# A residual block on one core: constant products in TensorE's first gaps, later norm steps on GpSimd, both middle rows in one addition

## The chip, the core and the metric

The kernel runs on one core of one Trainium2 chip. The metric is the device time of one execution in microseconds (us). The engines are named as in the profile: PE (TensorE, matmuls; PEld are its weight loads), DVE (VectorE), ACT (ScalarE), POOL (GpSimd) and SP (SyncE, which here issues DMAs).

## What is computed

The reference is a residual block of a diffusion model, for two images of 512 channels and 64 x 64 points, in bf16:

```python
def gn(z, gamma, beta):                       # 4 groups of 128 channels
    zr = z.reshape(B, G, (C // G) * H * W)
    mu = zr.mean(-1).reshape(B, G, 1)
    var = ((zr - mu) ** 2).mean(-1).reshape(B, G, 1)
    zn = ((zr - mu) / jnp.sqrt(var + eps)).reshape(B, C, H, W)
    return zn * gamma.reshape(1, C, 1, 1) + beta.reshape(1, C, 1, 1)
...
h = conv3(_silu(gn(x, g1, be1)), w1)          # 3 x 3, 512 -> 512 channels, zero padding
emb = _silu(t_emb) @ w_emb
h = h + emb.reshape(B, C, 1, 1)
h = conv3(_silu(gn(h, g2, be2)), w2)
return x + h
```

## The kernel before

**Tiling.** Channels lie on the 128 partitions, so there are four channel tiles (ct for input, ot for output), and a norm's group is one such tile. Each image is cut into two chunks of 32 rows; with two images that makes four chunks per layer, handled in order. A chunk and an output tile make one set (`one_set`): 16 sets in each of two layers, the very last of which is written out apart (`final_set`).

**The convolution.** Rows are transformed in the manner of Winograd: four output rows come from six positions (`pos` 0 to 5). `v_block` makes the transformed input V of one channel tile: ACT's SiLU with the norm's scale `sc` and bias `nb` writes `a_tmp`, and DVE additions (with some ACT or DVE scalings) turn that into V. `u_blocks` transposes the weights on PE and makes the transformed weights U on DVE and ACT. PE then multiplies V by U in `row_pair` and `col_pair` (the matmuls of L645, 512 or 256 columns wide, into three PSUM accumulators `acc`). `one_set` puts the output rows together: ACT copies accumulators to `m1`, `w_` and `mb`, DVE forms sums and differences in `w_`, ACT scales two of them by 2 and by 4 into the halves of `m1`, and DVE adds these to `w_` and so writes the middle output rows 1 and 2 of every four (two additions of 512 elements), then rows 0 and 3.

**Norms.** Image 0's first norm (`first_stats`) gets its sums of squares from PE products of x with itself (L943), its means from ACT and DVE sums or from PE products with ones (L957). Image 1's (`second_stats`) comes from ACT and DVE sums over 4096 elements (L985). Layer 1's norms (`stats2`) come from sums that layer 0's steps leave behind. All end in `norm`: a product with `ones_neg` (L405) sums over partitions, DVE copies it (L409), and a row of steps on numbers of one column per group (tile `arena`) makes `sc` and `nb`; two of the kinds of step run on POOL, the addition of epsilon (L419) and the power of minus one half (L423), the others on DVE.

**Order.** No queue's order is written out by hand. Every step is added to `_Plan` with an engine, a modelled cost and latency, what it reads and writes, and for PE's matmuls a due time. `issue` schedules all engines by lists with random restarts and then emits each engine's instructions in the order found. An engine works its queue strictly in that order, so one changed step or cost can change the order of everything. In the profile, L320, L325, L333 and L350 are the helpers `tt`, `ts`, `stt` and `act`, which record most DVE and ACT steps; steps are told apart there by tiles.

Of the kernel before, what the change touches and what calls it, by code (L numbers as in the profile page):

```python
# [12 lines left out]
ALU = mybir.AluOpType  # L13
# [11 lines left out]
class _Plan:  # L25
# [33 lines left out]
    def region(self, a):  # L59
        if isinstance(a, str):  # L60
            return a, 1
        m = self.mask(a.offset, tuple((d[0], d[1]) for d in list(a.ap)[1:]))
        bank = self.banks.get(a.tensor.name)
        if bank:
            m = sum(1 << i for i in range(8) if (m >> (i * bank)) & ((1 << bank) - 1))
        return a.tensor.name, m
# [124 lines left out]
def kernel(  # L191
# [13 lines left out]
    nc = tc.nc  # L205
    P = nc.NUM_PARTITIONS
# [20 lines left out]
    SMALLS = 344  # L227
    PARAM_LAND = 5.5
    LATE = 4.0
    DVE_SUMS = (1,)  # L230
    COL0 = (1, 2, 3)
    POS_ORDER = (1, 3, 2, 4, 0, 5)
# [85 lines left out]
    def tt(out, in0, in1, op, **kw):  # L318
        plan.add("DVE", vcost("tt", (out, in0, in1)),
                 lambda: nc.vector.tensor_tensor(out=out, in0=in0, in1=in1, op=op), [in0, in1], [out], **kw)  # L320
# [73 lines left out]
    sc_all = {(l, b): small([CT], "sc") for l in range(2) for b in range(B)}  # L394
    nb_all = {(l, b): small([CT], "nb") for l in range(2) for b in range(B)}

    def norm(layer, b, c0, n, me, ps=None):
        bank = None
        if ps is None:
            bank = XBank("xb", [2 * n], F32)  # L400
        tok = ["xb"] if ps is None else []

        def mm():
            o = ps if ps is not None else bank.get()[:]
            nc.tensor.matmul(o, lhsT=ones_neg[:], rhs=me[:], start=True, stop=True)  # L405
        plan.add("PE", 0.15, mm, [me[:], ones_neg[:]], tok if ps is None else [ps], lat=0.2, lead=100.0,
                 wait=0.05 if ps is not None else LATE)
        tot = small([2 * n], "tot")
        plan.add("DVE", 0.1, lambda: nc.vector.tensor_copy(out=tot[:], in_=ps if ps is not None else bank.get()[:]),  # L409
                 tok if ps is None else [ps], [tot[:]])  # L410
        nvar, rstd = small([n], "nvar"), small([n], "rstd")
        mu, ex = tot[:, 0:n], tot[:, n:2 * n]
        if n == 1:
            stt(nvar[:], mu, mu, ex, ALU.mult, ALU.add)
        else:
            tt(nvar[:], mu, mu, ALU.mult)
            tt(nvar[:], nvar[:], ex, ALU.add)
        ts(nvar[:], nvar[:], 0.0, op=ALU.min)
        pool(lambda: nc.gpsimd.tensor_scalar(out=rstd[:], in0=nvar[:], scalar1=-1.0, scalar2=EPS,  # L419
                                             op0=ALU.mult, op1=ALU.add), [nvar[:]], [rstd[:]])  # L420
        for i in range(n):
            r = rstd[:, i:i + 1]
            pool(lambda r=r: nc.gpsimd.tensor_tensor(out=r, in0=r, in1=neg_half[:], op=ALU.pow), [r, neg_half[:]], [r])  # L423
        sc, nb = sc_all[layer, b][:, c0:c0 + n], nb_all[layer, b][:, c0:c0 + n]
        tt(sc, rstd[:], gam(layer)[:, c0:c0 + n], ALU.mult)
        if layer == 1:
            tt(mu, mu, emb_sb[:, b, c0:c0 + n], ALU.add)
        if n == 1:
            stt(nb, mu, sc, bet(layer)[:, c0:c0 + n], ALU.mult, ALU.add)
        else:  # L430
            tt(nb, mu, sc, ALU.mult)
            tt(nb, nb, bet(layer)[:, c0:c0 + n], ALU.add)

    Ut = [[[None] * CT for _ in range(CT)] for _ in range(2)]
    KP = NKX * P
# [338 lines left out]
    def one_set(layer, idx, ot, U, V):  # L774
        b, ch = chunks[idx]
        col = is_col(layer, b, ch)
        more = layer == 1 and idx >= len(chunks) - 2
        gid = (layer, idx, ot)
        rows = slice(ch * CR * W, (ch + 1) * CR * W)
        yst = next_y()  # L780
        y4 = yst[:].rearrange("p (t f w) -> p f t w", f=TH, w=W)
        base = sum(cols_of(b, c) for c in range(ch))
        acc_sum = lambda i: ssum[b][:, ot, base + i:base + i + 1]

        late = more and idx == len(chunks) - 1 and ot == 0

        def first_pair():
            if more:
                (more_cols(U, V, gid) if idx == len(chunks) - 2 else more_pair(U, gid))
            else:  # L790
                a = row_pair((1, 3), U, V, col, gid, 1)
                if layer == 0:
                    act(m1[:], a[:], func=ACT.Identity, scale=KAPPA, accum=acc_sum(0))
                else:
                    act(m1[:], a[:], scale=KAPPA)

        if not late:
            first_pair()
        if col:
            ab = col_pair((1, 2), U, V, gid)  # L800
            act(mb[:].rearrange("p k j n -> p j k n"), ab, scale=0.5)
        a = row_pair((2, 4), U, V, col, gid, 1)
        act(w_[:, 1], a[:], scale=KAPPA)
        if late:
            first_pair()
        if col:
            tt(sd[:, 0], mb[:, 0], mb[:, 1], ALU.add)
            tt(sd[:, 1], mb[:, 0], mb[:, 1], ALU.subtract)
        tt(w_[:, 0], m1[:], w_[:, 1], ALU.add)
        tt(w_[:, 1], m1[:], w_[:, 1], ALU.subtract)  # L810
        t1, s1, t2, s2 = w_[:, 0, 0], w_[:, 1, 0], w_[:, 0, 1], w_[:, 1, 1]
        if layer == 0:
            act(m1[:, 1], t2, func=ACT.Identity, scale=4.0, accum=acc_sum(1))
            act(m1[:, 0], s2, func=ACT.Identity, scale=2.0, accum=acc_sum(2))
        else:
            act(m1[:, 0], s2, scale=2.0)
            act(m1[:, 1], t2, scale=4.0)
        act(s2, s2, scale=8.0)
        z12 = t4(m1[:])
        tt(y4[:, 1], z12[:, 0], t4(w_[:, 1, 0:1])[:, 0], ALU.add)  # L820
        tt(y4[:, 2], z12[:, 1], t4(w_[:, 0, 0:1])[:, 0], ALU.add)
        tt(w_[:, :, 0], w_[:, :, 0], w_[:, :, 1], ALU.add)
        w03 = t4(w_[:, :, 0])
        if not col:
            a = row_pair((0, 5), U, V, col, gid, 1)
            m05 = view(sd, 0, [[NFREE, 2], [1, NFREE]])
            act(m05, a[:], func=ACT.Identity, accum=acc_sum(3))
            tt(y4[:, 0:TH:TH - 1], t4(m05), w03, ALU.add)
        else:
            aa = col_pair((0, 3), U, V, gid)  # L830
            if layer == 0:
                for j in range(2):
                    for k, op in ((0, 1.0), (1, -1.0)):
                        stt(view(yst, k + j * (TH - 1) * W, [[TH * W, TR], [2, W // 2]]),
                            aa[:, j, k].rearrange("p (t w) -> p t w", t=TR), op,
                            sd[:, k, j].rearrange("p (t w) -> p t w", t=TR), ALU.mult, ALU.add,
                            accum=acc_sum(3 + 2 * j + k), more=[aa])
            else:
                for k, op in ((0, ALU.add), (1, ALU.subtract)):
                    tt(view(yst, k, [[(TH - 1) * W, 2], [TH * W, TR], [2, W // 2]]),  # L840
                       sd[:, k].rearrange("p j (t w) -> p j t w", t=TR),
                       aa[:, :, k].rearrange("p j (t w) -> p j t w", t=TR), op)
        y03 = y4[:, 0:TH:TH - 1]
        if col:
            tt(y03, y03, w03, ALU.add)
        if layer == 0:
            dma(h_scr[b, ot][:, rows], yst[:], reads=[yst[:]], writes=[f"h{b}{ot}{ch}"])
            act(yst[:], yst[:], func=ACT.Square, scale=float(HW) ** -0.5, accum=ssq[b][:, ot, ch:ch + 1])
            return
        dma(yst[:], x_v[b, ot][:, rows], reads=[yst[:]], writes=[yst[:]], eng="POOL", accum=ALU.add)  # L850
        dma(out_v[b, ot][:, rows], yst[:], reads=[yst[:]], due=clock["t"] + 20)
# [67 lines left out]

    xt = [Vbuf[CT + ct][:, 0:HW] for ct in range(CT)]  # L920
    wload = [u_load(0, 0, ct, lead=900.0 - 200.0 * ct) for ct in range(2)]
    for ct in range(CT):
        n = 2 if ct in (0, CT - 1) else 1
        for k in range(n):
            o = xt[ct][:, k * HW // n:(k + 1) * HW // n]
            dma(o, x_v[0, ct][:, k * HW // n:(k + 1) * HW // n], writes=[o], lead=800.0 - 200.0 * ct)
# [6 lines left out]
    def first_stats(ct):  # L933
# [25 lines left out]
            plan.add("PE", 1.8, colsum, [xt[ct], ones_bf[:]], [cs], lat=0.2)  # L959
            act(cs, cs, func=ACT.Identity, scale=1.0 / (P * HW), accum=me[:, 0:1])  # L960
        stt(gr, gr, 1.0 / HW, ident[:], ALU.mult, ALU.mult, accum=me[:, 1:2])
        norm(0, 0, ct, 1, me, ps=st[:, 0, 0:2])

    for ct in range(CT):
        first_stats(ct)
# [11 lines left out]
    def second_stats(ct):  # L977
# [4 lines left out]
        for k in range(2):  # L982
# [4 lines left out]
            else:  # L987
                act(src[0][:, 0:HW // 2], xin, func=ACT.Identity, accum=part[:, k:k + 1])
            act(src[0][:, 0:HW // 2], xin, func=ACT.Square, scale=float(HW) ** -0.5, accum=part[:, 2 + k:3 + k])
        stt(me[:, 0:1], part[:, 0:1], 1.0, part[:, 1:2], ALU.mult, ALU.add)  # L990
        ts(me[:, 0:1], me[:, 0:1], 1.0 / HW)
        tt(me[:, 1:2], part[:, 2:3], part[:, 3:4], ALU.add)
        norm(0, 1, ct, 1, me)

    for layer in range(2):
# [74 lines left out]
```

## Time and profile before

| | |
|---|---|
| median of 3 runs | 503.36 us (503.23 to 503.74) |
| the profiled execution | 503.6 us, of which its span from first to last instruction 501.7 us |
| mean granted PE clock | 0.995 |
| busy: PE, DVE, ACT, POOL | 479.1, 468.2, 398.3, 38.4 us |
| first L645 matmul | at 21.4 us |
| HBM read, written | 38.22 MB, 16.78 MB |

Times within the profile are counted from the span's first instruction. A row of the timeline gives start, duration, engine, line, operation, the tile written and those read, and in brackets the idle time of the engine just before with what ended it. Instructions of one engine can overlap a little, so that from start to start is less than the mean duration.

### The profile page before, as it was taken

The page shows a single profiled execution, that of the slowest core. Times are in us where ns is not written, and L with a number is a line of the kernel's source. Part 1 is how long each engine was busy: PE and PEld are TensorE (multiplying, and loading weights), DVE is VectorE, ACT ScalarE, POOL GpSimd, SP SyncE. Part 2 cuts the span into 40 slices and gives each one's busy share as a digit, 9 for nine tenths or more (in the row PEclk, how much of TensorE's full clock was granted, in tenths as well). Part 3 has the DMA queues.
Part 4 walks back from the last instruction along what each step waited for, and adds up shares of the span by engine and source line. Part 5 has one row for each costly group of instructions (what it writes and reads, how often), then busy time and mean ns, then how long its engine had stood idle before and what let it go on. Part 6 is the DMA issues. An engine that isn't in the chain of part 4 may idle for free.

```text
span 501.7 us, 8355 instructions
## 1 busy us (share of the span) xinstructions
PE 479.1 (95%) x3081; PEld 285.8 (57%) x3082; DVE 468.2 (93%) x1054; ACT 398.3 (79%) x548; POOL 38.4 (8%) x97
## 2 busy tenths in 40 slices
PE   5888999999999999999999999999999999999994
PEld 4654554455554555555665655555555666768572
DVE  3988999999999999899999999999999999998576
ACT  4888999999985895999999999767667867526362
POOL 1120000000110002000000000040010000000000
PEclk9999999999999999999999999999999999999998
DMA  8433233641210333222643122453626642424354
GB/s 301 178 77 92 69 106 121 220 181 43 78 51 2 109 105 110 86 86 89 179 137 114 67 86 51 120 129 84 171 43 151 187 125 47 127 62 107 85 125 127
DMA packets 17315, 55.53 MB, mean 111 GB/s; under 512 B 1915, under 2 KB 3067, under 8 KB 16507
## 3 DMA queue, kind: packets, MB, share of 16 engines
q1 hardware_dynamic: 14912, 46.86, 27.5%
q0 software_dynamic: 2160, 7.87, 9.5%
q8 instruction: 24, 0.39, 0.4%
q10 hardware_dynamic: 203, 0.27, 0.1%
q14 instruction: 16, 0.13, 0.1%
HBM read 38.22 MB, written 16.78 MB: 110 GB/s over the span
## 4 chain that ended last, share of the span: by engine, by line
PE 51%; DVE 18%; ACT 5%; POOL 1%; issue 1%; DVEq 0%
PE acc L645 50%; DVE V L320 4%; DVE vt L320 4%; DVE w L320 2%; DVE y L320 2%; DVE y L333 2%; ACT U L495 1%; POOL arena L423 1%; DVE sd L320 1%; DVE arena L985 1%; ACT a_tmp L350 1%; DVE vt L325 1%; PE xa L389 1%; ACT m L350 1%; POOL arena L419 1%
## 5 line engine op out<-in xcount | busy, mean ns | idle before, releaser
L645 PE MATMUL acc<-V,U 128*128 128x512 bf16 (+1 forms) x2400 | 435.1, 338 | 7.0 <-DVE V L320 3.2
L645 PEld LDWEIGHTS <-U 128*128 128x128 bf16 x2592 | 250.2, 98 | 186.2 <-issue 9.5
L320 DVE TENSOR_TENSOR V<-vt 128x1056 bf16<-128x1056 bf16 (+2 forms) x132 | 90.3, 691 | 3.6 <-ACT vt L350 1.2
L350 ACT ACTIVATE m<-w 128x512 bf16<-128x512 bf16 x62 | 38.1, 636 | 14.7 <-DVE w L320 14.6
L350 ACT ACTIVATE w<-acc 128x1024 bf16<-128x1024 f32 (+1 forms) x32 | 32.5, 1016 | 19.2 <-PE acc L645 7.8
L320 DVE TENSOR_TENSOR w<-m,w 128x1024 bf16<-128x1024 bf16 (+1 forms) x63 | 42.7, 679 | 5.0 <-ACT w L350 4.6
L350 ACT ACTIVATE src<-vt 128x528 bf16<-128x528 bf16 x54 | 34.6, 650 | 15.5 <-DVE vt L320 15.3
L320 DVE TENSOR_TENSOR U<-U 128x768 bf16<-128x768 bf16 (+2 forms) x96 | 45.1, 483 | 0.7 <-ACT U L495 0.5
L350 ACT ACTIVATE a_tmp<-src,arena 128x2112 bf16<-128x2112 bf16 x20 | 43.0, 2152 | 2.7 <-DVE stage L320 2.7
L350 ACT ACTIVATE mb<-acc 128x1024 bf16<-128x1024 f32 x32 | 32.8, 1024 | 12.4 <-PE acc L645 8.1
L320 DVE TENSOR_TENSOR vt<-a_tmp 128x1056 bf16<-128x1056 bf16 x56 | 39.0, 700 | 0.7 <-ACT a_tmp L350 0.4
L389 PEld LDWEIGHTS <-stage 128*128 128x128 bf16 x288 | 26.5, 144 | 12.5 <-DMA stage<-in_w_dram 3.8
L350 ACT ACTIVATE y<-y 128x2048 bf16<-128x2048 bf16 x16 | 30.6, 1909 | 0.0
L495 ACT COPY U<-xa 128x768 bf16<-128x768 bf16 x31 | 25.6, 826 | 3.8 <-PE xa L389 3.7
L320 DVE TENSOR_TENSOR sd<-mb 128x512 bf16<-128x512 bf16 x64 | 25.8, 417 | 2.4 <-ACT mb L350 2.4
L350 ACT ACTIVATE m<-acc 128x1024 bf16<-128x1024 f32 x24 | 24.6, 1025 | 3.4 <-DVE y L320 3.3
L350 ACT ACTIVATE a_tmp<-V,arena 128x2112 bf16<-128x2112 bf16 x12 | 26.0, 2169 | 1.6 <-DVE arena L333 1.6
L320 DVE TENSOR_TENSOR y<-m,w 128x512 bf16<-128x512 bf16 x62 | 24.7, 416 | 1.1 <-ACT m L350 0.7
L368 POOL DMA_DIRECT2D y<-in_x_dram x15 | 13.2, 879 | 149.6 <-DVE y L320 128.6
L564 POOL MEMSET a_tmp<- 128x64 bf16 x32 | 5.2, 167 | 241.3 <-DVE vt L320 213.9
L320 DVE TENSOR_TENSOR vt<-vt,a_tmp 128x1056 bf16<-128x1056 bf16 x32 | 22.4, 701 | 0.9 <-ACT vt L350 0.9
L350 ACT ACTIVATE src<-V 128x2048 bf16<-128x2048 bf16 x12 | 22.9, 1906 | 0.0
(115 smaller groups left out, 504.6 us busy)
## 6 DMA issues: line engine op xcount, KB each, us to landing
stage<-in_w_dram SPq DMA_DIRECT2D x32, 288.0 KB, 2.8
src<-h_scr SPq DMA_DIRECT2D x16, 528.0 KB, 3.8
h_scr<-y SPq DMA_DIRECT2D x16, 512.0 KB, 3.0
y<-in_x_dram POOLq DMA_DIRECT2D x15, 512.0 KB, 5.6
out_dram<-y SPq DMA_DIRECT2D x15, 512.0 KB, 2.9
V<-in_x_dram SPq DMA_DIRECT2D x6, 1024.0 KB, 6.8
src<-in_x_dram SPq DMA_DIRECT2D x4, 528.0 KB
V<-in_x_dram SPq DMA_DIRECT2D x4, 512.0 KB, 6.9
```

The costliest lines, as they stand in the source:

```text
L320: lambda: nc.vector.tensor_tensor(out=out, in0=in0, in1=in1, op=op), [in0, in1], [out], **kw)
L325: nc.vector.tensor_scalar(out=out, in0=in_, scalar1=c, scalar2=None, op0=op)
L333: nc.vector.scalar_tensor_tensor(out=out, in0=in0, scalar=scalar, in1=in1, op0=op0, op1=op1, **extra)
L350: nc.scalar.activation(out=out, in_=in_, func=fn, scale=scale, **extra)
L368: q.dma_start(out=out, in_=in_, **extra)
L389: nc.tensor.transpose(sel(t), in_, ident[:in_.shape[0], :in_.shape[0]])
L419: pool(lambda: nc.gpsimd.tensor_scalar(out=rstd[:], in0=nvar[:], scalar1=-1.0, scalar2=EPS, op0=ALU.mult, op1=ALU.add), [nvar[:]], [rstd[:]])
L423: pool(lambda r=r: nc.gpsimd.tensor_tensor(out=r, in0=r, in1=neg_half[:], op=ALU.pow), [r, neg_half[:]], [r])
L495: lambda: nc.scalar.copy(out=out, in_=sel(bank.get())), [tok], [out])
L564: pool(lambda r=r: nc.gpsimd.memset(rows[:, r, 1:W + 1], 0.0), [], [rows[:, r, 1:W + 1]], cost=0.2)
L645: nc.tensor.matmul(ap, lhsT=l, rhs=r, start=k == 0, stop=k == total[key] - 1)
L985: plan.add("DVE", 2.18, lambda xin=xin, o=part[:, k:k + 1]: nc.vector.reduce_sum(out=o, in_=xin, axis=AX.X), [xin], [part[:, k:k + 1]])
```

## The change

It has four parts.

1. 23 groups of two 128 x 128 products of a tile of ones with itself are added for PE, into `acc[2]`, whose contents nothing reads; 11 of the groups depend on nothing else, 12 on the first weight block having landed.
2. The small steps of `norm` are written anew. The fused DVE steps (`stt`) become two plain ones each; the clamp takes the sign along, and the addition of epsilon is a POOL step of its own. With `quick=True` (image 0's first norms) the plain steps stay on DVE; otherwise they run on POOL. The planner's cost of a power step is 0.7 us instead of 0.45.
3. In `second_stats` three DVE steps become two POOL steps.
4. In `one_set` the two additions for output rows 1 and 2 become one of 1024 elements, which reads the two halves of `w_` with a negative step in its outermost dimension. `region`, with which the planner finds dependences, learns negative steps.

```diff
+        dims = [(d[0], d[1]) for d in list(a.ap)[1:]]
+        first = a.offset + sum(step * (n - 1) for step, n in dims if step < 0)
+        m = self.mask(first, tuple((abs(step), n) for step, n in dims))
...
+    WARM = (11, 12)
...
-        if n == 1:
-            stt(nvar[:], mu, mu, ex, ALU.mult, ALU.add)
-        else:
-            tt(nvar[:], mu, mu, ALU.mult)
-            tt(nvar[:], nvar[:], ex, ALU.add)
-        ts(nvar[:], nvar[:], 0.0, op=ALU.min)
-        pool(lambda: nc.gpsimd.tensor_scalar(out=rstd[:], in0=nvar[:], scalar1=-1.0, scalar2=EPS,
-                                             op0=ALU.mult, op1=ALU.add), [nvar[:]], [rstd[:]])
+        def two(out, in0, in1, op, fast=False):
+            if fast:
+                tt(out, in0, in1, op)
+            else:
+                pool(lambda: nc.gpsimd.tensor_tensor(out=out, in0=in0, in1=in1, op=op), [in0, in1], [out])
+
+        two(nvar[:], mu, mu, ALU.mult, quick)
+        two(nvar[:], nvar[:], ex, ALU.add, quick)
+        pool(lambda: nc.gpsimd.tensor_scalar(out=nvar[:], in0=nvar[:], scalar1=0.0, scalar2=-1.0,
+                                             op0=ALU.min, op1=ALU.mult), [nvar[:]], [nvar[:]])
+        pool(lambda: nc.gpsimd.tensor_scalar(out=rstd[:], in0=nvar[:], scalar1=EPS, scalar2=None, op0=ALU.add),
+             [nvar[:]], [rstd[:]])
...
-        tt(sc, rstd[:], gam(layer)[:, c0:c0 + n], ALU.mult)
+        two(sc, rstd[:], g_, ALU.mult, quick)
         if layer == 1:
-            tt(mu, mu, emb_sb[:, b, c0:c0 + n], ALU.add)
-        if n == 1:
-            stt(nb, mu, sc, bet(layer)[:, c0:c0 + n], ALU.mult, ALU.add)
-        else:
-            tt(nb, mu, sc, ALU.mult)
-            tt(nb, nb, bet(layer)[:, c0:c0 + n], ALU.add)
+            two(mu, mu, emb_sb[:, b, c0:c0 + n], ALU.add)
+        two(nb, mu, sc, ALU.mult, quick)
+        two(nb, nb, b_, ALU.add, quick)
...
-        tt(y4[:, 1], z12[:, 0], t4(w_[:, 1, 0:1])[:, 0], ALU.add)
-        tt(y4[:, 2], z12[:, 1], t4(w_[:, 0, 0:1])[:, 0], ALU.add)
+        tt(y4[:, 1:3], t4(m1[:]), view(w_, 2 * NFREE, [[-2 * NFREE, 2], [W, TR], [1, W]]), ALU.add)
...
+    for after in [()] * WARM[0] + [(wload[0][:, 0:1],)] * WARM[1]:
+        plan.add("PE", 0.2, lambda: [nc.tensor.matmul(acc[2][:, 1, 0:P], lhsT=ones_bf[:], rhs=ones_bf[:], start=True,
+                                                      stop=True) for _ in range(2)],
+                 [ones_bf[:]] + list(after), [acc[2][:]], group=("warm",), lat=0.1, due=4.0, lead=-100.0)
...
-        stt(me[:, 0:1], part[:, 0:1], 1.0, part[:, 1:2], ALU.mult, ALU.add)
-        ts(me[:, 0:1], me[:, 0:1], 1.0 / HW)
-        tt(me[:, 1:2], part[:, 2:3], part[:, 3:4], ALU.add)
+        pair = me[:, 0:2]
+        pool(lambda: nc.gpsimd.tensor_tensor(out=pair, in0=part[:, 0:4:2], in1=part[:, 1:4:2], op=ALU.add),
+             [part[:, 0:4]], [pair])
+        pool(lambda: nc.gpsimd.tensor_scalar(out=me[:, 0:1], in0=me[:, 0:1], scalar1=1.0 / HW, scalar2=None,
+                                             op0=ALU.mult), [me[:, 0:1]], [me[:, 0:1]])
```

More of the change, by code (lines that the diff above doesn't have):

```diff
@@ L61, in region @@
             return a, 1
-        m = self.mask(a.offset, tuple((d[0], d[1]) for d in list(a.ap)[1:]))
+        dims = [(d[0], d[1]) for d in list(a.ap)[1:]]
+        first = a.offset + sum(step * (n - 1) for step, n in dims if step < 0)
+        m = self.mask(first, tuple((abs(step), n) for step, n in dims))
         bank = self.banks.get(a.tensor.name)
@@ L395, with norm @@
     nb_all = {(l, b): small([CT], "nb") for l in range(2) for b in range(B)}
-    def norm(layer, b, c0, n, me, ps=None):
+    def norm(layer, b, c0, n, me, ps=None, quick=False):
         bank = None
@@ L412, in norm @@
         mu, ex = tot[:, 0:n], tot[:, n:2 * n]
-        if n == 1:
-            stt(nvar[:], mu, mu, ex, ALU.mult, ALU.add)
-        else:
-            tt(nvar[:], mu, mu, ALU.mult)
-            tt(nvar[:], nvar[:], ex, ALU.add)
-        ts(nvar[:], nvar[:], 0.0, op=ALU.min)
-        pool(lambda: nc.gpsimd.tensor_scalar(out=rstd[:], in0=nvar[:], scalar1=-1.0, scalar2=EPS,
-                                             op0=ALU.mult, op1=ALU.add), [nvar[:]], [rstd[:]])
+        sc, nb = sc_all[layer, b][:, c0:c0 + n], nb_all[layer, b][:, c0:c0 + n]
+        g_, b_ = gam(layer)[:, c0:c0 + n], bet(layer)[:, c0:c0 + n]
+        def two(out, in0, in1, op, fast=False):
[9 more added lines that the diff above has]
+             [nvar[:]], [rstd[:]])
         for i in range(n):
             r = rstd[:, i:i + 1]
-            pool(lambda r=r: nc.gpsimd.tensor_tensor(out=r, in0=r, in1=neg_half[:], op=ALU.pow), [r, neg_half[:]], [r])
-        sc, nb = sc_all[layer, b][:, c0:c0 + n], nb_all[layer, b][:, c0:c0 + n]
-        tt(sc, rstd[:], gam(layer)[:, c0:c0 + n], ALU.mult)
+            pool(lambda r=r: nc.gpsimd.tensor_tensor(out=r, in0=r, in1=neg_half[:], op=ALU.pow), [r, neg_half[:]], [r],
+                 cost=0.7)
+        two(sc, rstd[:], g_, ALU.mult, quick)
         if layer == 1:
-            tt(mu, mu, emb_sb[:, b, c0:c0 + n], ALU.add)
-        if n == 1:
-            stt(nb, mu, sc, bet(layer)[:, c0:c0 + n], ALU.mult, ALU.add)
-        else:
-            tt(nb, mu, sc, ALU.mult)
-            tt(nb, nb, bet(layer)[:, c0:c0 + n], ALU.add)
+            two(mu, mu, emb_sb[:, b, c0:c0 + n], ALU.add)
+        two(nb, mu, sc, ALU.mult, quick)
+        two(nb, nb, b_, ALU.add, quick)
     Ut = [[[None] * CT for _ in range(CT)] for _ in range(2)]
@@ L818, in one_set @@
         act(s2, s2, scale=8.0)
-        z12 = t4(m1[:])
-        tt(y4[:, 1], z12[:, 0], t4(w_[:, 1, 0:1])[:, 0], ALU.add)
-        tt(y4[:, 2], z12[:, 1], t4(w_[:, 0, 0:1])[:, 0], ALU.add)
+        tt(y4[:, 1:3], t4(m1[:]), view(w_, 2 * NFREE, [[-2 * NFREE, 2], [W, TR], [1, W]]), ALU.add)
         tt(w_[:, :, 0], w_[:, :, 0], w_[:, :, 1], ALU.add)
@@ L961, in first_stats @@
         stt(gr, gr, 1.0 / HW, ident[:], ALU.mult, ALU.mult, accum=me[:, 1:2])
-        norm(0, 0, ct, 1, me, ps=st[:, 0, 0:2])
+        norm(0, 0, ct, 1, me, ps=st[:, 0, 0:2], quick=True)
     for ct in range(CT):
```

## The prediction

> **What bounds the kernel now.** I began with the page's first block and the chain that ended last.
>
> ```profile
> PE 479.1 (95%) x3081; PEld 285.8 (57%) x3082; DVE 468.2 (93%) x1054; ACT 398.3 (79%) x548; POOL 38.4 (8%) x97
> PE 51%; DVE 18%; ACT 5%; POOL 1%; issue 1%; DVEq 0%
> ```
>
> Two engines are nearly full, and the chain names both. An average can't say which of them a change must relieve, so the next view is the busy time by stage (columns: PE, PEld, DVE, ACT, POOL with counts, clock, DMA).
>
> ```profile
> 0.00:20.00 20.00, 12.99 (x131) 10.69 (x133) 11.14 (x41) 11.34 (x14) 3.49 (x28) 1.00 0.77 285
> 20.00:60.00 40.00, 35.39 (x256) 20.73 (x255) 36.14 (x89) 35.41 (x54) 4.15 (x10) 1.00 0.30 82
> 110.00:160.00 50.00, 48.23 (x277) 26.69 (x275) 48.78 (x134) 45.57 (x56) 6.23 (x11) 1.00 0.12 43
> 330.00:440.00 110.00, 110.00 (x698) 67.66 (x697) 109.73 (x214) 78.69 (x92) 10.43 (x19) 1.00 0.46 120
> 491.00:501.70 10.70, 3.19 (x21) 1.75 (x19) 6.79 (x16) 3.43 (x6) 0.00 (x0) 0.78 0.53 147
> ```
>
> TensorE loses time in the first 60 us, loses little in the middle, nothing from 330 to 440, and then the tail runs on DVE and ACT. So DVE time saved late is worth nothing; saved early it is worth what TensorE waits for. The waits of TensorE over the whole run (waiter, releaser: us, times, longest):
>
> ```profile
> PE xa L389 <- DMA stage<-in_w_dram: 3.8, 1, 3.8
> PE acc L645 <- DVE V L320: 3.2, 4, 1.7
> PE acc L405 <- DVE acc L333: 1.9, 2, 1.1
> PE acc L645 <- DVE y L333: 1.8, 2, 1.1
> PE acc L645 <- ACT mb L350: 1.4, 2, 0.8
> PE xb L916 <- DMA stage<-in_w_dram: 1.2, 1, 1.2
> PE acc L943 <- DMA V<-in_x_dram: 0.8, 1, 0.8
> ```
>
> With three small ones these make 14.8 us. 5.8 us wait for DMA at the start. Some 5.6 us (3.2 + 1.9 + 0.3 + 0.2) wait for the DVE chain before 60 us. Only 3.4 us lie after 60 us: 1.8 on L333, 1.4 on mb, 0.2 on m. That is the whole pot. The sum is made against the profiled execution, 503.6 us (span 501.7 and 1.9 around it), 0.24 above the median of 503.36.
>
> **Part 1, products in the first gaps.** 23 groups of two products of ones. In the built order 32 stand ahead of the first six transposes and 14 more up to the second weight block's. The timeline of the start:
>
> ```profile
> 5.43 1.89 PE L943 MATMUL acc<-V 128*128 128x128 bf16 x16 [0.79 <-DMA V<-in_x_dram]
> 8.58 1.89 PE L943 MATMUL acc<-V 128*128 128x128 bf16 x16
> 12.29 1.95 PE L943 MATMUL acc<-V 128*128 128x128 bf16 x32
> 14.54 2.15 ACT L350 ACTIVATE a_tmp<-V,arena 128x2112 bf16<-128x2112 bf16 x1 [1.58 <-DVE arena L333]
> ```
>
> Sixteen products take 1.89 us early and thirty-two take 1.95 us at 12.29: 118 against 61 ns each. TensorE starts at half rate and comes to full rate 3.8 us after it resumed at 8.45; the first burst, 3.8 to 7.3 with a gap, did not bring it. With products from about 1.2 us on (the constants are written by then) it has been at work over 5 us when the first image block's products end at about 6.4 us. It then idles some 2 us until the second half lands at 8.58; the trace has TensorE waits up to 1.7 us with no fall in rate. I take it that the rate is up by then and stays up. The Trainium skill (TensorE: Matmul & The Clock Gate, What's actually happening) says that a window of about 3.4 us of work releases the clock and a whole idle window takes it back, the windows running free of the kernel's start; by that rule the rate holds over a 2 us gap, and the 3.8 us seen here agrees.
>
> Cost: 22 products at 118 ns are 2.6 us, ending at 3.8 us beside the 3.8 us wait for the weights. Ten more wait for the weights and put the first transposes back by up to 1.2 us, of which the faster transposes (0.85 us now, about 0.5 later in the trace) return 0.35. DVE has 2.9 us of idle time behind its use of them, so I cost this at nothing; without that cover it is 0.8 us.
>
> Gain on the chain to the first SiLU: the second sixteen end near 9.56 and not 10.47, but DVE's partial sum ends at 9.99, so DVE's step that reads the products out (L333 on acc, now at 10.58) moves by 0.6, not 0.9. The product with ones_neg runs 0.38 us for 0.59, another 0.2. So −0.8 to there.
>
> **Part 2, the first image's norms (quick).** Per channel tile one more GpSimd step and one more small DVE step (4 to 5). In this chain one GpSimd step lies 0.48 us ahead of the next (12.87 to 13.35), 0.27 in the third tile (25.09 to 25.36). One small DVE step more is 0.15 for a dependent one, less 0.07 as plain additions are shorter than the fused form (0.15 against 0.22). So +0.35 to +0.6: the first SiLU comes 0.2 to 0.5 us earlier. The built order also puts the second tile's trace product and norm ahead of four V steps of some 0.6 us; walking the DVE rows in that order with the durations of the trace, I get the second SiLU 1.0 us earlier than its 22.86. Against that, later first-image V steps move back. Part 1 and 2 together: between +0.3 and −1.7; I take −0.7, the middle, since the rows of DVE until 46 us sum to the same work.
>
> **Part 3, later norms to GpSimd.** For each of the four norms of image 1 seven small DVE rows go. From start to start between 104 and 122 us they take 0.07, 0.07, 0.06, 0.13, 0.06, 0.07 and 0.13: 0.59 each, 2.4 us. Two DVE waits for the power step (0.23 at 127.83, 0.72 at 145.27) go as well. Each of the two second-layer norms loses seven rows, 0.5 us each. GpSimd gets 8 more steps per norm of image 1. The steps it has now:
>
> ```profile
> L419 POOL TENSOR_SCALAR arena<-arena x10: 191/568/1765, 12.9 to 327.9; 128x1 f32<-128x1 f32 x8, 128x4 f32<-128x4 f32 x2
> ```
>
> A chain of eight steps from mean to nb at 0.57 and some 0.1 between is 5.4 us. The last channel tile now takes 5.8 (141.87 to 147.66) with DVE's queue in it. At the median this is even. Behind the norm steps on GpSimd stand only the memsets of a_tmp's edges in layer 0, which ACT's SiLU waits for; in layer 1 y's accumulating transfers, which seven more steps put back by some 4 us once; the three y buffers hide that, and without them it is a DVE wait of that size. No transfer is added; the new lines in region serve only the planner's bookkeeping.
>
> **Part 4, the middle rows in one addition.** The two forms exist in the trace apart from the negative step:
>
> ```profile
> L320 DVE TENSOR_TENSOR y<-m,w 128x512 bf16<-128x512 bf16 x62 | 24.7, 416 | 1.1 <-ACT m L350 0.7
> L320 DVE TENSOR_TENSOR y<-sd,w 128x1024 bf16<-128x1024 bf16 x4 | 2.7, 682 | 0.0
> ```
>
> Instructions overlap: two of the first kind take 0.67 us from start to start (156.78 to 157.45), one of the second 0.60. So 0.07 us a set, 31 sets, 2.2 us, not the 4.7 that the means suggest; about 0.6 before 151 us. The negative step is on the outermost dimension, the 64 inner elements still run forward, and no row shows one. Upper bound: a f32 PSUM addition of 512 takes 0.72, so 1024 at that rate are about 1.3, +0.7 a set. I take the fast end, as every row with forward runs of 64 bf16 is fast. The merged addition also has to await both ACT scalings (0.5 us apart); the order has other rows between.
>
> **Sum.** By 151 us DVE is freed of 2.4 + 0.95 + 0.6 = 3.9 us. TensorE's wait for L333 at 151 us was 1.1 and at 208 us 0.7: both go, −1.8. The mb waits (1.4) are ACT's and stay. Nearly the whole order of all queues is chosen anew, so new waits come, 0 to 2 us; I take +0.5, the size of the small ones now. −0.7 − 1.8 + 0.5 = −2.0: 501.6 profiled, 501.4 median. The tail's own steps are not touched.
>
> **Rivals.** *GpSimd starves (slower).* The step at 142.84 took 1.77 us and ended when DVE ran dry at 144.55: it got through only in a DVE gap. The change takes away just those gaps. If four of the last tile's steps take 1.77, its SiLU comes 4.8 us late; with about 2 us of slack TensorE waits 2.8 more, and the 1.8 isn't won: −0.7 + 2.8 = +2.1, 505.5. It decides from two starved steps on. Against it: the median 0.57, and three steps at 0.19. The Trainium skill (SBUF — State Buffer, SBUF: two separate sides) speaks for it: a DVE step with two SBUF inputs and a GpSimd step that reads SBUF exclude each other for the whole instruction. The 1.77 agrees; DVE rows beside GpSimd steps aren't longer here (0.69 at 112.11).
>
> *The order gives it back (no change).* The rate doesn't rise early (the gap at 6.4 cools it), or new waits reach 2 us: 502.4 to 504.4, centre 503.4.
>
> *The negative step is slow (slower).* +0.7 on some 16 sets in layer 0 is 11 us of DVE, less 5 freed; a good half reaches TensorE: +3.5, 507.
>
> *All early waits move (faster).* −1.7 − 3.4 with no new wait: 498.3.
>
> **Chances.** Forecast (500.2 to 502.4) 0.54; starved 0.16; given back 0.20; slow step 0.04; larger gain 0.06. A measurement of this kernel tells about 0.2%, 1.0 us, from no change. Faster 0.60, same 0.20, slower 0.20. The range 499.2 to 504.8 leaves out the slow step, most of the starved case and half of the larger gain.
>
> **What would show it.** In the timeline of the start: sixteen products at about 1 us at 8.6, L333 on acc near 10.0, first SiLU near 14.2. In the lines by form: y<-m,w 128x1024 x31 near 680 ns; near 1300 it is the slow step. PE waits on y L333 near 151 gone. GpSimd arena steps: median under 0.6; over 1.0 between 110 and 150 us, with ACT's a_tmp waiting for POOL, means starvation. A rise in PE waits after 60 us above 3.4 us makes the forecast wrong.

## The result and the profile after

The changed kernel takes 504.92 us (median of 14 runs, 503.33 to 506.79), the kernel before, beside it on the same chips, 503.28 us. The ratio is 1.0035, 95% interval 1.0022 to 1.0048: slower by 1.6 us, where 501.4 was forecast. It also spreads more than before: 3.5 us from lowest to highest against 1.5. The profiled execution took 505.68 us, span 503.9.

The busy times, and the stages that answer to those shown of before (columns PE, PEld, DVE, ACT, POOL, clock, DMA share, GB/s):

```profile
PE 483.2 (96%) x3128; PEld 288.9 (57%) x3128; DVE 463.4 (92%) x985; ACT 398.6 (79%) x548; POOL 72.0 (14%) x147
```

```profile
0.00:20.00 20.00, 15.82 (x177) 13.81 (x178) 10.22 (x40) 10.09 (x12) 3.78 (x29) 0.91 0.77 285
20.00:60.00 40.00, 37.63 (x281) 22.21 (x280) 36.75 (x95) 37.98 (x59) 6.59 (x13) 1.00 0.33 89
110.00:160.00 50.00, 49.78 (x288) 27.93 (x287) 49.76 (x118) 46.37 (x58) 16.75 (x38) 1.00 0.15 54
260.00:330.00 70.00, 67.17 (x424) 39.34 (x423) 65.38 (x150) 61.20 (x86) 20.27 (x17) 1.00 0.29 77
330.00:440.00 110.00, 107.61 (x664) 64.90 (x664) 107.55 (x197) 74.71 (x91) 8.02 (x15) 0.98 0.47 118
```

The stretch from 260 to 330 us of the kernel before:

```profile
260.00:330.00 70.00, 69.98 (x444) 40.70 (x443) 69.66 (x169) 63.02 (x89) 4.40 (x7) 1.00 0.30 85
```

DVE did get work taken off: 463.4 us for 468.2. In the middle PE is fuller than before (49.78 against 48.23 us from 110 to 160). But from 260 to 330 us, where PE had been full, 2.8 us are missing, from 330 to 440 another 2.4, and the granted clock there is 0.98. POOL is at work for 20 us between 260 and 330, with 17 instructions. The waits of PE, up to 60 us and then from 60 us on:

```profile
PE xb L921 <- DMA mb<-in_g_dram: 2.1, 1, 2.1
PE acc L652 <- DVE V L323: 1.7, 1, 1.7
PE acc L928 <- DVE ones_bf L903: 1.1, 1, 1.1
PE acc L408 <- DVE acc L336: 0.6, 1, 0.6
```

```profile
PE acc L652 <- ACT mb L353: 5.4, 4, 4.9
PE acc L652 <- DVE V L323: 0.4, 1, 0.4
PE acc L652 <- ACT w L353: 0.4, 1, 0.4
```

(The lines have moved: L645 is now L652, L320 L323, L333 L336, L350 L353; in an experiment with more lines of its own they lie a little further on.) The waits on DVE before 60 us fell from 5.6 to 2.8 us (1.7 + 0.6 + 0.3 + 0.2, the last two not shown), not counting the 1.1 us until the tile of ones is written, for which nothing waited before. After 60 us all but one wait make 1.3 us, against 3.4. That one, 4.9 us, stands at 327 us. Back from there, first POOL, then ACT:

```profile
309.74 0.20 POOL L423 TENSOR_TENSOR arena<-arena,emb_sb 128x4 f32<-128x4 f32 x1
310.04 10.13 POOL L427 TENSOR_SCALAR arena<-arena 128x4 f32<-128x4 f32 x1
320.25 0.24 POOL L429 TENSOR_SCALAR arena<-arena 128x4 f32<-128x4 f32 x1
320.57 5.49 POOL L433 TENSOR_TENSOR arena<-arena,neg_half 128x1 f32<-128x1 f32 x4
...
326.71 0.20 POOL L423 TENSOR_TENSOR arena<-arena,gb 128x4 f32<-128x4 f32 x1
```

```profile
320.23 1.02 ACT L353 ACTIVATE w<-acc 128x1024 bf16<-128x1024 f32 x1 [1.80 <-PE acc L652]
326.94 2.15 ACT L353 ACTIVATE a_tmp<-src,arena 128x2112 bf16<-128x2112 bf16 x1 [5.69 <-POOL arena L423]
...
331.01 1.00 ACT L353 ACTIVATE mb<-acc 128x1024 bf16<-128x1024 f32 x1
...
332.43 1.00 ACT L353 ACTIVATE m<-acc 128x1024 bf16<-128x1024 f32 x1
```

This is the second image's layer 1 norm. Its clamp, a step on 4 columns that takes 0.2 to 0.3 us where it is quick, took 10.13 us. Of the four power steps the first took 3.94 us, the others 0.54 each. ACT's SiLU needs the norm and stood in ACT's queue 5.69 us; behind it stood the copy `mb` that empties an accumulator for PE. PE waited for that, and its granted clock then fell to half for one stretch of 3.4 us: the eleven matmuls from 332.06 us on took 4.23 us, some 1.7 more than at the 0.21 us from one to the next that they take afterwards. What DVE ran meanwhile:

```profile
309.38 0.71 DVE L323 TENSOR_TENSOR y<-sd,acc 128x512 bf16<-128x512 bf16 x1
310.00 0.66 DVE L323 TENSOR_TENSOR w<-m,w 128x1024 bf16<-128x1024 bf16 x1
310.59 0.69 DVE L323 TENSOR_TENSOR V<-vt 128x1056 bf16<-128x1056 bf16 x1
...
319.38 0.67 DVE L323 TENSOR_TENSOR y<-y,w 128x1024 bf16<-128x1024 bf16 x1
319.98 0.71 DVE L323 TENSOR_TENSOR y<-sd,acc 128x512 bf16<-128x512 bf16 x1
```

From 310.00 to 319.98 stand twenty additions, one behind the other, each with both inputs in SBUF. The clamp ended 0.2 us after the first addition that reads PSUM had begun. The slow power step ended the same way, 0.5 us after the next such addition had begun at 324.00.

Adding up against before: waits on DVE before 60 us −2.8, other waits after 60 us −2.1, the new wait +4.9, half rate +1.7. That is +1.7 us. The two profiled spans differ by 2.2 us, the medians by 1.6; waits for DMA, the time of the added products and the tail are not in the sum.

### The profile page after: what moved, and what is told of

Same layout as the page of the kernel before. It is cut to its first block, busy times and chain, and to the rows that moved or that the text cites. A ratio compares the mean times of both kernels' runs of the same rounds, so it can differ in the third digit from the quotient of the medians.

```text
span 503.9 us, 8459 instructions
## 1 busy us (share of the span) xinstructions
PE 483.2 (96%) x3128; PEld 288.9 (57%) x3128; DVE 463.4 (92%) x985; ACT 398.6 (79%) x548; POOL 72.0 (14%) x147
## 5 line engine op out<-in xcount | busy, mean ns | idle before, releaser
L652 PE MATMUL acc<-V,U 128*128 128x512 bf16 (+1 forms) x2400 | 437.7, 339 | 8.1 <-ACT mb L353 5.4
L652 PEld LDWEIGHTS <-U 128*128 128x128 bf16 x2592 | 250.3, 98 | 187.9 <-issue 12.5
L323 DVE TENSOR_TENSOR V<-vt 128x1056 bf16<-128x1056 bf16 (+2 forms) x132 | 89.9, 693 | 5.2 <-PE acc L652 2.6
L353 ACT ACTIVATE mb<-acc 128x1024 bf16<-128x1024 f32 x32 | 32.7, 1021 | 24.4 <-PE acc L652 16.6
L353 ACT ACTIVATE a_tmp<-src,arena 128x2112 bf16<-128x2112 bf16 x20 | 42.9, 2146 | 7.0 <-POOL arena L423 5.7
L353 ACT ACTIVATE w<-acc 128x1024 bf16<-128x1024 f32 (+1 forms) x32 | 32.4, 1013 | 19.6 <-PE acc L652 15.2
L323 DVE TENSOR_TENSOR w<-m,w 128x1024 bf16<-128x1024 bf16 (+1 forms) x63 | 42.9, 681 | 3.9 <-ACT w L353 3.4
L353 ACT ACTIVATE m<-w 128x512 bf16<-128x512 bf16 x62 | 37.2, 624 | 10.1 <-DVE w L323 10.0
L323 DVE TENSOR_TENSOR U<-U 128x768 bf16<-128x768 bf16 (+2 forms) x96 | 44.8, 485 | 0.4
L323 DVE TENSOR_TENSOR vt<-a_tmp 128x1056 bf16<-128x1056 bf16 x56 | 38.9, 701 | 2.3 <-ACT a_tmp L353 2.0
L353 ACT ACTIVATE src<-vt 128x528 bf16<-128x528 bf16 x54 | 34.2, 641 | 8.4 <-DVE vt L323 8.4
L353 ACT ACTIVATE y<-y 128x2048 bf16<-128x2048 bf16 x16 | 30.6, 1917 | 0.0
L371 POOL DMA_DIRECT2D y<-in_x_dram x15 | 13.3, 887 | 113.2 <-DVE y L323 103.1
L323 DVE TENSOR_TENSOR sd<-mb 128x512 bf16<-128x512 bf16 x64 | 26.1, 418 | 1.7 <-ACT mb L353 1.7
L353 ACT ACTIVATE a_tmp<-V,arena 128x2112 bf16<-128x2112 bf16 x12 | 25.8, 2151 | 2.1 <-DVE arena L323 2.1
L353 ACT ACTIVATE m<-acc 128x1024 bf16<-128x1024 f32 x24 | 24.6, 1024 | 2.9 <-DVE y L323 2.2
L323 DVE TENSOR_TENSOR y<-sd,acc 128x512 bf16<-128x512 bf16 (+1 forms) x34 | 22.7, 688 | 3.9 <-PE acc L652 3.7
L353 ACT ACTIVATE src<-V 128x2048 bf16<-128x2048 bf16 x12 | 22.9, 1906 | 0.6 <-DMA V<-in_x_dram 0.6
L323 DVE TENSOR_TENSOR vt<-vt,a_tmp 128x1056 bf16<-128x1056 bf16 x32 | 22.5, 703 | 0.8 <-ACT vt L353 0.8
```

The costliest lines, as they stand in the source:

```text
L353: nc.scalar.activation(out=out, in_=in_, func=fn, scale=scale, **extra)
L371: q.dma_start(out=out, in_=in_, **extra)
L652: nc.tensor.matmul(ap, lhsT=l, rhs=r, start=k == 0, stop=k == total[key] - 1)
```

## The experiments

All kernels named "same order" keep the order of every queue of the changed kernel; only what the diff shows differs. The ratios are to the kernel before, run beside them.

**1. Layer 1's norm steps back on DVE, same order** (`l1_dve_same_order`)

```diff
+        small_eng = nc.vector if layer == 1 else nc.gpsimd
...
-                pool(lambda: nc.gpsimd.tensor_tensor(out=out, in0=in0, in1=in1, op=op), [in0, in1], [out])
+                pool(lambda: small_eng.tensor_tensor(out=out, in0=in0, in1=in1, op=op), [in0, in1], [out])
```

> The changed kernel with every queue's order kept; only the small steps of layer 1's two norms (not the power) run on DVE instead of GpSimd. Theory A (starvation): the clamp step of image 1's layer 1 norm took 10.1 us on GpSimd while DVE ran additions with two SBUF inputs one behind the other, ACT's SiLU stood 5.7 us behind it, PE 4.9 us, and PE's rate was halved for 3.4 us after that (7 products lost 0.21 us each, 1.5 us). Taken away, 504.9 - 4.9 - 1.5 = 498.5 us (498 to 499.5, ratio to before 0.990 to 0.993), no PE wait on mb near 327 us. Theory B (order): the newly chosen order gives the gain back, and the slow step only fills a wait that is there anyway: 504 to 505.

Measured: 501.69 us, ratio 0.9965 (0.9953 to 0.9976). Both theories missed the size: 3.2 us came back, half of the 6.4 that theory A expected. The power steps, still on POOL, show why:

```profile
310.85 5.27 POOL L434 TENSOR_TENSOR arena<-arena,neg_half 128x1 f32<-128x1 f32 x4 [2.19 <-DVE arena L430]
```

```profile
PE acc L653 <- ACT m L353: 2.5, 1, 2.5
```

Four power steps took 5.27 us in the same place, PE waited 2.5 us, and the half rate came again. The first of the four took 3.72 us and ended at 314.57, when DVE had run out of additions (the last ended at 314.15). The other three took 0.54 us each, while DVE stood idle: its next step, the product with the power, waited 2.01 us for them. So PE's wait comes here by way of DVE's queue. The slow thing is any GpSimd step beside those additions, not the moved ones alone; and the edit has a cost of its own, DVE's wait for the power.

**2. One-column writes between DVE's additions, same order** (`breathers_same_order`)

```diff
         for i in order:
             nodes[i].emit()
+            if getattr(nodes[i], "mark", 0):
+                left = 45
+            elif left and nodes[i].eng == "DVE":
+                self.breathe()
+                left -= 1
...
         two(nvar[:], mu, mu, ALU.mult, quick)
+        if layer == 1 and b == 1:
+            plan.nodes[-1].mark = 1
...
+    plan.breathe = lambda: nc.vector.memset(pad[:, 0:1], 0.0)
```

> The changed kernel with every queue's order kept; behind each of the 45 DVE steps that follow the first step of image 1's layer 1 norm stands one more, a write of one column to a tile that nothing reads. DVE gets more work (45 x 0.06 = 2.7 us) and is no less busy. Theory A (starvation by two-input additions one behind the other): GpSimd gets in between, its steps there fall below 1 us each, PE's wait of 4.9 us goes, 498.5 to 500.5 us. Theory A2 (GpSimd waits until DVE is idle, whatever DVE runs): the clamp still takes about 10 us or longer, 505 to 507.5 us. Theory B (order): no gain, 504.5 to 507.

Measured: 497.85 us (496.90 to 499.58), ratio 0.9885 (0.9868 to 0.9902). More work on DVE made the kernel 7.1 us faster than the changed one, of which the wait and the half rate are 6.6. (Between the two profiles another 2.5 us lie at the start, where this one's rate held; the writes, which begin at 306 us, have no part in that.) The same steps on POOL, and DVE beside them:

```profile
307.41 0.26 POOL L435 TENSOR_SCALAR arena<-arena 128x4 f32<-128x4 f32 x1
307.75 0.70 POOL L437 TENSOR_SCALAR arena<-arena 128x4 f32<-128x4 f32 x1
308.53 2.52 POOL L441 TENSOR_TENSOR arena<-arena,neg_half 128x1 f32<-128x1 f32 x4
```

```profile
307.66 0.69 DVE L329 TENSOR_TENSOR w<-m,w 128x1024 bf16<-128x1024 bf16 x1
307.70 0.06 DVE L927 MEMSET pad<- 128x1 f32 x1
308.27 0.70 DVE L329 TENSOR_TENSOR V<-vt 128x1056 bf16<-128x1056 bf16 x1
```

The clamp takes 0.26 us for 10.13, four power steps 2.5 for 5.5. DVE is as full as ever (11.00 of 11 us from 307 to 318), so theory A2 (POOL waits for an idle DVE) falls, and with it theory B (the order, and not the slow step, costs the time): the order is the same. What it is in a write that lets the step in is not shown. A write adds next to nothing between large additions: from one to the next it is 0.61 us with it, 0.59 to 0.60 without.

**3. No products of ones, same order** (`no_products_same_order`; the two matmuls of each added group are left out)

> The changed kernel with every other instruction and order kept, without the 46 products of ones. In the trace of the changed kernel the granted clock fell to half from 8.1 to 11.5 us, so the second sixteen products of L952 ran at 1.9 us as before. If the products are worth nothing for that reason: 504.9 within 0.5 us. If they are worth the 0.7 us that the prediction gave the start: 505.6. If they hold up the first products (six places behind them at half rate): 504.2.

Measured: 504.89 us, ratio 1.0029 (1.0017 to 1.0040), as with them (1.0035). On the median the products are worth nothing that can be told. The changed kernel's timeline shows what became of them in the profiled execution:

```profile
5.54 1.07 PE L952 MATMUL acc<-V 128*128 128x128 bf16 x16 [0.34 <-DMA V<-in_x_dram]
8.73 0.17 PE L921 MATMUL xb<-ident,mb 16*128 16x16 bf16 x1 [2.12 <-DMA mb<-in_g_dram]
8.83 0.61 PE L928 MATMUL acc<-ones_bf 128*128 128x128 bf16 x4
9.23 1.91 PE L952 MATMUL acc<-V 128*128 128x128 bf16 x16
```

The rate was up at 5.5 us (1.07 us for sixteen) and down again at 9.2 (1.91). The products meant for the gap stood in PE's queue behind L921, a transpose that waited 2.1 us for the norm parameters' DMA, so they filled nothing. In the profiled execution of experiment 4, whose start has the same instructions, that wait was 1.0 us, the rate held, and the first L652 matmul began at 19.9 us; here it began at 21.5, without products at 20.7. In these three profiles, that is, the products bring the start forward where the rate holds and put it back where the rate falls. The mean granted clock suggests which was the rule: it is 0.989 in the profiled execution, with two stretches at half rate ahead of the tail, and no higher than 0.990 in ten of the fourteen runs (504.3 to 506.8 us). The other four have 0.992 or 0.993 and took 503.3 to 504.7. That goes some way to explain the wide spread.

**4. Two additions for rows 1 and 2, same order** (`two_additions_same_order`; the lines of before in the place of the one addition)

> The changed kernel with every order kept, but output rows 1 and 2 by two additions of 512 elements in the place of the one of 1024 (no negative step). 31 more DVE steps, 0.07 us each by the trace of before: 2.2 us of DVE, of which some 1.2 lie before 330 us. Theory A says that PE is what counts and DVE's small savings show only where PE waits: 504.9 to 505.9. If the negative step were slow in some way that the mean of 686 ns does not show, the time would fall below 504.5.

Measured: 505.18 us, ratio 1.0035 (1.0019 to 1.0050), the same as with one addition. The merged addition is worth nothing that can be measured here; its own price is as forecast:

```profile
L323 DVE TENSOR_TENSOR y<-m,w 128x1024 bf16<-128x1024 bf16 x31 | 21.3, 686 | 1.5 <-ACT m L353 1.0
```

686 ns: the negative outer step costs nothing.

**5. The first gap filled** (`breathers_filled`: experiment 2 with 36 more products straight behind the first sixteen of L952, ahead of L921)

> The kernel with one-column writes between DVE's additions, and 36 more products of ones straight behind the first sixteen products of the first image block, ahead of the parameters' transpose, where PE stood still for 0.3 to 2.1 us. In the traces so far the rate fell again after that gap in two runs and held in two; where it held the second sixteen products took 1.07 us and not 1.9, and the first L652 matmul began at 19.9 us and not at 21.5. If the gap makes it fall: the rate holds in every run, the first L652 matmul at about 19.5 us, 496.5 to 497.7 us with a smaller spread than the 2.7 us of the kernel without the 36. If the rate's fall has nothing to do with the gap, or the start does not reach the end: 497.9 within 0.5. If the products come too late and hold up the second block: 498.5.

Measured: 497.94 us (497.58 to 498.14), ratio 0.9896 (0.9884 to 0.9909). The median stays, the spread falls from 2.7 us to 0.6 in the few runs there are. In its profile the second sixteen products take 1.06 us, but they began only at 9.5 us (7.8 in experiment 2's profile): the 36 products ahead of them ended at 9.2, and the second half of x came late, too, as ACT's first step on it began at 9.0 (7.9 there). The rate held here, and by the mean granted clock (0.995 to 0.997) in all four runs. But it held in experiment 2's profile, too; that the 36 products are what holds it, or that they pay, is not shown.

**6. Image 1's layer 0 norm steps back on DVE** (`breathers_image1_dve`: experiment 2, with the diff of experiment 1 for `layer == 0 and b == 1`)

> The kernel with one-column writes, every queue's order kept, with the norm steps of image 1's layer 0 norms (not the power, not the two steps on the sums) on DVE again, at the places where the planner had them on GpSimd. 28 small DVE steps more between 105 and 150 us, 2 to 3 us, and DVE waits for the power steps. If relief of DVE there is what took away PE's waits of 1.1 us at 151 us and 0.7 at 208 us (the prediction's step): 498.9 to 500 us. If PE has slack there in this order: 497.9 within 0.5.

Measured: 502.15 us (499.26 to 504.17), ratio 0.9973 (0.9955 to 0.9991): 4.3 us of the gain go, more than expected. Between the two profiles lie 5.3 us, and 2.4 of them lie at the start, ahead of all that the edit touches: the first L661 matmul began at 21.4 us, against 19.0; the rate fell again. Later PE has two new waits, the first ending at 145.6 us, the second at 135.8, and GpSimd shows what made the longer one:

```profile
PE xb L415 <- POOL arena L1013: 1.7, 1, 1.7
PE acc L661 <- DVE arena L438: 0.9, 1, 0.9
```

```profile
138.77 6.74 POOL L1013 TENSOR_SCALAR arena<-arena 128x1 f32<-128x1 f32 x1
```

L1013 is one of the two steps on the sums that stay on GpSimd. It took 6.74 us beside DVE's additions (0.57 for the same step in experiment 2), and PE's product for the next norm waited for it, with all matmuls behind. That is the slow GpSimd step again, here in layer 0. The shorter wait is DVE's, whose queue holds the small steps again; DVE itself waited for GpSimd nowhere between 60 and 200 us. So only some 0.9 us of the loss speak for the relief of DVE that the prediction counted on. What that relief is worth is not shown by this run.

**7. Other orders** (`before_seed2` to `4`, `after_seed2` to `4`: another seed of the planner's random restarts; same instructions)

> The kernel before with another seed of the planner's random restarts: same instructions, another order of all queues. Tells what the order alone is worth. If the order is a small matter: 503.5 within 1 us. If the 5.7 us between the kernel with one-column writes and the kernel before could come from a lucky order: a change of 3 us or more, either way.

> The changed kernel with another seed of the planner's random restarts. If GpSimd's starvation lies in any order of this change (layer 1's DVE work is nearly all additions with two SBUF inputs): a GpSimd step of several us there again, a PE wait of 2 to 6 us, 502 to 507 us. If the first order was bad luck: no GpSimd step over 2 us that ACT waits for, 497 to 500 us.

> The kernel before, planner's seed 3. Seeds 1 and 2 gave 503.3 and 500.5 us. If the order is worth some 3 us: 499.5 to 504.

> The changed kernel, planner's seed 3. Seeds 1 and 2 gave 504.9 and 499.0 us. If the change is worth 2 us of itself, as the sum of the prediction had it, and starvation strikes only where ACT's SiLU stands close behind the norm: 497.5 to 500 without a PE wait on it near 310 to 330 us, 502 to 506 with one.

> The kernel before, planner's seed 4: 499.5 to 504 us, as for seed 3.

> The changed kernel, planner's seed 4: as for seed 3, 497.5 to 500 us without a PE wait behind GpSimd's norm steps of layer 1, 502 to 506 with one. If the change is worth nothing of itself, the four orders of each kernel have means within 1 us.

| seed | before, us | ratio | changed, us | ratio |
|---|---|---|---|---|
| 1 | 503.28 | 1 | 504.92 | 1.0035 (1.0022 to 1.0048) |
| 2 | 500.53 | 0.9952 (0.9940 to 0.9964) | 499.04 | 0.9923 (0.9903 to 0.9944) |
| 3 | 505.27 | 1.0030 (1.0016 to 1.0044) | 502.53 | 0.9983 (0.9967 to 1.0000) |
| 4 | 501.66 | 0.9960 (0.9947 to 0.9972) | 499.29 | 0.9935 (0.9902 to 0.9967) |

The order alone moves the kernel before by 4.7 us and the changed one by 5.9. The means are 502.7 and 501.4. With three of four seeds the change is faster, by 1.5 to 2.7 us, with the first it is slower. The mean difference, −1.2 us, is a little over the 1 us named beforehand for a change worth nothing of itself, but with so few orders it is not told apart from none; the spread by seed is about as large as the forecast gain. Seed 3's changed kernel shows the same wait again, ACT first, then PE:

```profile
331.06 2.15 ACT L353 ACTIVATE a_tmp<-src,arena 128x2112 bf16<-128x2112 bf16 x1 [3.07 <-POOL arena L423]
```

```profile
PE acc L652 <- ACT m L353: 2.5, 1, 2.5
```

In seed 2 a GpSimd step takes 4.4 us, too, in image 1's layer 0 (from 127.8 us on); ACT's SiLU waits 2.4 us for that norm, but PE has no wait on ACT there. In seed 4 it is again a layer 0 norm of image 1, and there PE pays 2.0 us, from 153.5 us on:

```profile
145.55 3.85 POOL L423 TENSOR_TENSOR arena<-arena 128x1 f32<-128x1 f32 x2 [5.84 <-DVE arena L412]
```

```profile
152.38 2.15 ACT L353 ACTIVATE a_tmp<-V,arena 128x2112 bf16<-128x2112 bf16 x1 [4.82 <-POOL arena L423]
```

```profile
PE acc L652 <- ACT mb L353: 2.2, 2, 2.0
```

The first of those two steps took 3.58 us. So where a GpSimd step is slow, and who pays for it, changes with the order.

**8. The writes in seed 3** (`breathers_seed3`)

> The changed kernel with planner's seed 3 and a one-column write behind each of 45 DVE steps from the first step of image 1's layer 1 norm on. Without the writes this order took 502.5 us; four power steps took 5.6 us at 324 us, ACT's SiLU waited 3.1 us for GpSimd and PE 2.5 us for ACT, with 3.4 us at half rate some us later. If that wait is starvation: no such wait, 499 to 500.5 us. If the order of seed 3 is slow for other reasons: 502.5 within 0.7.

Measured: 498.39 us, ratio 0.9906 (0.9879 to 0.9934), for 502.5 without them. From 60 to 485 us PE stands idle for 0.5 us in all, against 2.9 without the writes, and the rate stays whole there. The slow GpSimd steps are what made this order slow, too.

**9. The writes in the kernel before** (`before_breathers`)

> The kernel before with one-column writes behind DVE steps from the clamp of every norm on but image 0's first. There GpSimd's norm steps are two and not ten or more, and PE waits for none of them after 60 us. If the writes help only where GpSimd's steps are waited for: 503.5 within 0.7. If they help in some other way (as in the changed kernel): 500 or less.

Measured: 505.79 us, ratio 1.0046 (1.0028 to 1.0064): slower by 2.3 us. So they do not help by themselves; they help where POOL is waited for. Here they stand behind small steps, too, where each costs: from a small step to the next row it is 0.14 to 0.15 us with a write between and 0.07 without. DVE is full between 110 and 160 us, and PE's waits on ACT's mb and on DVE there grow from 1.7 to 2.7 us. The rest of the 2.3 us was not followed up.

**10. Versions made from what was found** (`best_seed2`, `best_seed4`: seeds 2 and 4, writes behind 45 DVE steps from the first GpSimd step of every norm but image 0's, the gap filled)

> A version made from what was found: the changed kernel, planner's seed 2, one-column writes behind 45 DVE steps from the first GpSimd step of each norm on but image 0's, and 36 more products in the first gap. Seed 2 without them: 499.0 us, with no PE wait behind GpSimd over 0.8 us. If both help where there is something to take: 497 to 498.5. If the writes or products cost: 499 to 500.

> The same with planner's seed 4 (499.3 us without them; the profiled execution shows 6.8 us at half rate from 8.3 us on, and a PE wait of 2.0 us at 153 us on ACT, whose queue is behind image 1's norm). If the rate holds and that wait goes: 496 to 497.5 us. If not: 498.5 to 499.5.

Measured: 498.74 us, ratio 0.9908 (0.9893 to 0.9924), and 500.66 us, 0.9954 (0.9937 to 0.9970). Seed 2 is as it was; seed 4's median is 1.4 us above that without, which the intervals don't tell apart. Both miss what was expected. In seed 4's profile the rate holds and the wait of 2.0 us is gone, as hoped for, but three waits on DVE, where a write is the step named, make 0.9 us. The writes in the stage of image 1's norms, among small steps, probably cost what experiment 9 shows; that was not tried apart. The fastest kernels found are experiments 2 and 5, 497.9 us, which beat both kernels given.

## Why the prediction was wrong, by its own steps

**The step that failed is part 3's "at the median this is even".** It priced GpSimd's chain by the median step, 0.57 us, and compared it in the stage of image 1's layer 0 norms. There it held: the POOL chains at 107 to 149 us ran about as reckoned (4.6 to 5.6 us each for 5.4), and PE's wait at 151 us went. It was applied unchanged to layer 1's norms, where DVE's work is of another kind. In this order layer 0 mixes sums and PSUM reads into DVE's queue where GpSimd's steps stand; layer 1 runs up to twenty two-input additions in a row there. The row that should have warned stood in the prediction itself, 191/568/1765: a spread of nine times is no size for a sum. The clamp there took 10.13 us, the first power step behind it 3.94.

**The second fault is in the same part: who waits.** "In layer 1 y's accumulating transfers" named what stands behind the norm in POOL's queue. What counted is who needs its result, ACT's SiLU, and what stands behind that in ACT's queue, the accumulator's copy. The price came as 4.9 us of PE wait and 1.7 us of half rate, which the sum had at nothing. Experiment 2, with the order kept, gives them back.

**The rival "GpSimd starves" had the mechanism and nearly the time** (505.5 against 504.9). The time is luck: its sum was made for another place, 110 to 150 us, with a wait of 2.8 us, and in this order the starved steps stood at 310 to 325 us, so its chance of 0.16 was weighed by the wrong rows. In seed 4's order the named place was right (3.58 us at 145.6, PE 2.0 us behind it). Experiments 2 and 8 show the mechanism. The page of the Trainium skill named there (SBUF — State Buffer, SBUF: two separate sides) agrees in kind: two-input DVE steps shut out a GpSimd step that reads SBUF. It says that whichever starts first has the ports; the measured 10.13 us show that the waiting step does not get its turn between twenty such additions, and the measurement decides.

**Part 1's −0.8 to the first SiLU** did not come in the profiled run. That the rate would rise early was right (1.07 us at 5.5 us). That it would hold over a gap of 2 us was wrong there: it fell at 8.1 us, in a gap of 2.1; in experiment 4's profile, with a gap of 1.0, it held. The rule given in part 1 has it hold over both gaps; the measurement decides. Where the products stand in the queue was in the built order, L921 ahead of four of them, and was not weighed.

**Part 2's first SiLU** came at 15.7 us, not 14.2, in the profiled run (13.3 in experiment 2's, where the rate held and the second half of x landed sooner). The second SiLU came at 23.1, not 21.9. What was gained before 60 us is in PE's waits on DVE, 2.8 us less, more than the 1.7 at the far end of the range given.

**The middle, −1.8 and +0.5,** −1.3 net, came out at −2.1 without the one long wait. **Part 4** was right in price (686 ns) and right that little follows.

**The sum as a whole** left out how far an order can move the kernel, 4.7 us from seed to seed with nothing changed. A re-planned kernel needs that in its range. Nor was the rest of the sum right for this order: without the long wait and the half rate it takes 497.9 us (experiment 2), 3.5 below the forecast. How much of that is the change and how much the order stays open.

## What to carry to other kernels

A small step on GpSimd is priced by what DVE runs beside it, not by its median: look for unbroken runs of two-input additions in DVE's queue, and ask who waits for the step and what is queued behind that waiter. If such a step must stay, a one-column write between the large additions let it in here; in the kernel before, where nothing waited for such a step, the writes cost 2.3 us. And where a planner makes the order, compare several orders of each version before a change of under one per cent is called a gain or a loss.

## What the runs showed of the hardware that was not expected

- A GpSimd step of 0.26 us took 10.13 us beside twenty DVE additions with two SBUF inputs, and the four power steps 5.5 us, 3.9 of them the first; with 0.06 us one-column writes between the additions they took 0.26 and 2.5 us.
- The slow steps ended when DVE came to an addition that reads PSUM (begun at 319.98 and 324.00 us, ends at 320.17 and 324.51) or ran dry (experiment 1: at 314.15, end at 314.57). Two scalings with one input, at 143.25 and 144.55 us of experiment 6, did not end the 6.74 us of L1013.
- DVE's additions were no slower beside waiting GpSimd steps (those of 1024 and 1056 elements 0.66 to 0.69 us from 310 to 320 us).
- PE's rate fell to half for 3.4 us in the stretch from 8.1 to 11.5 us of the changed kernel's profile, although PE had worked 1.6 of the 3.4 us before it; in another profile of the same start, where its wait was 1.0 us and not 2.1, it did not fall.
